# Converting 64-bit weights to 32 bits: one of three VectorE passes given to GpSimd

## Chip, cores and metric

One NeuronCore of a Trainium2 chip runs the whole kernel. The metric is the device time of one execution in microseconds. The median of three executions of the kernel before is 675.44 us (668.51 to 679.55).

## What is computed

The reference has two parts. The first is a causal attention with a memory term, for 4 batches of 8 heads, 576 rows each, head width 64, in fp32:

```python
scores = scale * np.matmul(q, k.transpose(0, 1, 3, 2))      # causal mask, softmax over the last axis
local = np.matmul(a, v)
mem_out = einsum(phi(q), M_prev) / (einsum(phi(q), z_prev) + 1e-06)
attn = g * mem_out + (1 - g) * local
```

The second is a dense layer pair on the 2304 rows of that result: `h = x @ w_in`, `g = s * relu(h)**2 + b`, `out = g @ w_out`, with w_in of 512 x 2048 and w_out of 2048 x 512. Both weight matrices arrive as 64-bit floats. TensorE takes 32-bit operands, so the kernel turns each 64-bit number into a 32-bit one on the chip before it uses it.

## The kernel before

**Conversion.** A 64-bit number arrives as two 32-bit words, `lo` and `hi`, side by side in a tile of 128 rows x 512 numbers x 2 words (`xa` for w_in, `raw` for w_out). `conv64` (lines 73 to 85) makes 32-bit floats from it. ScalarE reads `hi` as a float and scales it by a power of two, which moves the exponent to its 32-bit place (line 82). VectorE shifts the result left by three bits (line 83), brings the top three bits of `lo` in at the bottom (line 84, a shift of `lo` by 29 and an or), and sets the sign from `hi` (line 85). Line 83 reads one operand, lines 84 and 85 two each.

**Who calls it.** `split_w` converts w_in in 16 pieces of 128x512 during the first stage. After each piece, GpSimd rounds the result to the matmul's operand type (line 470, the high half) and VectorE subtracts to get the low half (line 471). `conv_u` converts w_out in 16 pieces while the last hidden-layer matmuls run; its results go through `t_u` and `split_u` on VectorE and ScalarE.

**Stages.** From 17 to 155 us the kernel handles the first four head pairs: scores on TensorE (L295, L300, L301), a masked minimum on VectorE (L314), an exponential on ScalarE (L322), the row sums' reciprocal on VectorE (L329, L330), the normalization of P on GpSimd (L334, for each head one instruction per row tile), transposes of P on TensorE (L373), and the product with V (L405 to L408). The 16 conversions of w_in are spread over this stage. The first hidden-layer matmul (L482) starts at 122 us. From 155 to 412 us attention of the later batches and hidden-layer matmuls share TensorE. From 412 to 476 us only hidden-layer matmuls are left, and w_out is converted beside them. From 477 us on the second layer runs (L744 to L746).

**What sets the order.** Every engine executes its own queue in order. The program gives the work in an order written by hand (a table of times), and a scheduler then places each instruction on its engine's queue by its own simulated times. An instruction inside `pin(...)` keeps its place relative to the other pinned ones; the others are free to move. SyncE (SP) issues the loads, also in order. A piece's load goes into one of four `xa` tiles, so load n waits until an earlier conversion has read its tile for the last time, at line 85. The loads are numbered here as the pieces are, from 0: loads 0 to 3 need no tile freed, load 7 needs the line 85 of piece 3, load 10 that of piece 7, load 11 that of piece 9, load 13 that of piece 11.

Of the kernel before, what the change touches and what calls it, by code (L numbers as in the profile page):

```python
# [12 lines left out]
ALU = mybir.AluOpType  # L13
# [18 lines left out]
def attention_moe_kernel(  # L32
# [15 lines left out]
    nc = tc.nc  # L48
# [26 lines left out]
    def conv64(raw, w, pin=lambda x: x):  # L75

        lo, hi = raw[:, :, 0], raw[:, :, 1]  # L80
        wu = w.bitcast(U32)
        pin(nc.scalar.activation(w, hi.bitcast(F32), AF.Abs, scale=2.0 ** -112))
        pin(nc.vector.tensor_scalar(wu, wu, 3, None, ALU.logical_shift_left))
        nc.vector.scalar_tensor_tensor(wu, lo, 29, wu, ALU.logical_shift_right, ALU.bitwise_or)
        nc.vector.scalar_tensor_tensor(wu, hi, 0x80000000, wu, ALU.bitwise_and, ALU.bitwise_or)


# [46 lines left out]
    pin = tc.keep_in_program_order  # L134
# [326 lines left out]
    def split_w(n):  # L461
        c, p = divmod(n, NP)
        cs = slice(512 * (c % 2), 512 * (c % 2) + 512)
        w = ap1.tile([128, 512], F32, tag="w", name="w", bufs=2)
        conv64(st.pop(("wst", n)), w, pin if PINC else same)
        H, L = (t[:, p, cs] for t in W[c // 2])
        if T["wa"][n]:
            nc.scalar.copy(H, w)
        else:
            nc.gpsimd.tensor_scalar(H, w, 1.0, 1.0, ALU.mult, ALU.mult)  # L470
        nc.vector.tensor_sub(L, w, H.bitcast(F32))
# [179 lines left out]
    def conv_u(n):  # L651
        i, h = divmod(n, 2)
        if h == 0:
            st["b"] = stage(i)
        w, s = st["b"]
        conv64(st.pop(("u", n)), w[:, 2 * h:2 * h + 2].rearrange("p a b -> p (a b)"))
        if n in NEXT:
            for r in NEXT[n]:
                load_u(r)
        if h == 0:  # L660
            return
        later(2, t_u, i, w, s)
        later(4, split_u, i, w, s)
# [223 lines left out]
```

## Time and profile before

| | |
|---|---|
| median of 3 executions | 675.44 us |
| the profiled execution | 674.27 us |
| its span, first to last instruction | 672.5 us |
| mean granted TensorE clock | 0.982 |
| busy: TensorE, VectorE, ScalarE, GpSimd | 634.5, 485.1, 469.0, 356.6 us |

The page of the profile gives each engine's busy time over the whole span. The stages differ: TensorE is busy all the time from 412 to 470 us, and less so in the first stage, where its matmuls wait for the other engines. So the windows are read by stage, then the waits inside a stage, then the lines. PE is TensorE, DVE VectorE, ACT ScalarE, POOL GpSimd, and SP the queue of SyncE that issues the loads.

### The profile page before, as it was taken

Reading aid. Unit: us, or ns where it says so; the run is one execution under the profiler, and the core shown is the slowest. Engines: PE = TensorE matmul, PEld = TensorE weight load, DVE = VectorE, ACT = ScalarE, POOL = GpSimd, SP = SyncE. Lnnn points to the kernel's source line nnn. Section 1 sums busy time; section 2 is a strip of 40 time slices with the busy share of each in tenths; the row PEclk is TensorE's granted clock in tenths of the full one; section 3 lists DMA queues with packets and bytes.
Section 4 is the critical chain, followed back from the end, with each engine's and each line's share of the span. In section 5 each row is a group of like instructions: output and inputs, shape, how many; then the busy total and the mean of one; then the engine's idle time right before and its main releaser. Section 6 shows DMA issues by size and latency. Waiting matters only on the chain. (4 is left out here: it accounts for less than half of the span.)

```text
span 672.5 us, 12998 instructions
## 1 busy us (share of the span) xinstructions
PE 634.5 (94%) x4536; PEld 575.9 (86%) x4536; DVE 485.1 (72%) x1109; ACT 469.0 (70%) x1053; POOL 356.6 (53%) x370
## 2 busy tenths in 40 slices
PE   5989799979999999999999999999899999999998
PEld 3545455869999999898998999999899998899998
DVE  4987778889677767866767653985977875568574
ACT  5677585767777767767767754769898768686841
POOL 1745556557646656654755331000577656665683
PEclk9998797999999999999999999999999999999999
DMA  7986876767778697786875564656653443434201
GB/s 268 267 232 156 177 189 157 200 170 209 190 204 214 173 231 194 201 220 173 204 189 133 140 221 142 212 189 235 227 150 118 131 137 98 125 95 156 95 25 40
DMA packets 73442, 115.75 MB, mean 172 GB/s; under 512 B 10016, under 2 KB 51232, under 8 KB 73376
## 3 DMA queue, kind: packets, MB, share of 16 engines
q1 hardware_dynamic: 71200, 112.55, 60.6%
q10 hardware_dynamic: 2176, 2.36, 1.0%
q8 instruction: 36, 0.59, 0.4%
q14 instruction: 30, 0.25, 0.1%
HBM read 57.68 MB, written 23.59 MB: 121 GB/s over the span
## 5 line engine op out<-in xcount | busy, mean ns | idle before, releaser
L334 POOL TENSOR_SCALAR P<-P,sm,omg 128x64 f32<-128x64 f32 (+4 forms) x136 | 94.7, 710 | 61.1 <-DVE sm L330 40.5
L322 ACT ACTIVATE P<-P,mn 128x64 f32<-128x64 f32 (+4 forms) x160 | 89.5, 560 | 36.1 <-DVE mn L314 35.5
L746 PE MATMUL yps<-bH,op 128*128 128x256 f32 x360 | 102.3, 285 | 2.9 <-DVE op L736 2.9
L744 PE MATMUL yps<-bH,op 128*128 128x256 f32 x360 | 101.9, 283 | 0.8 <-ACT r L491 0.8
L745 PE MATMUL yps<-bL,op 128*128 128x256 f32 x360 | 101.8, 283 | 0.0
L314 DVE CUSTOM_DVE_ANT_0 P<-sps,mask 128x64 f32<-128x64 f32 (+4 forms) x160 | 65.9, 423 | 28.8 <-PE sps L301 22.3
L373 PE MATMUL tps<-ident,P 128*128 128x128 f32 (+2 forms) x480 | 75.3, 278 | 4.7 <-POOL P L334 3.1
L482 PE MATMUL hps<-xs,w1H 128*128 128x320 f32 (+1 forms) x256 | 77.7, 304 | 0.9 <-DVE ptl L225 0.5
L482 PE MATMUL hps<-xs,w0H 128*128 128x320 f32 (+1 forms) x256 | 78.5, 307 | 0.0
L484 PE MATMUL hps<-xs,w0L 128*128 128x320 f32 (+1 forms) x256 | 75.9, 297 | 0.0
L484 PE MATMUL hps<-xs,w1L 128*128 128x320 f32 (+1 forms) x256 | 75.8, 296 | 0.0
L483 PE MATMUL hps<-xs,w0H 128*128 128x320 f32 (+1 forms) x256 | 75.8, 296 | 0.0
L483 PE MATMUL hps<-xs,w1H 128*128 128x320 f32 (+1 forms) x256 | 75.7, 296 | 0.0
L746 PEld LDWEIGHTS yps<-bH,op 128*128 128x128 f32 x360 | 68.5, 191 | 4.0 <-DVE op L736 3.9
L744 PEld LDWEIGHTS yps<-bH,op 128*128 128x128 f32 x360 | 68.6, 190 | 1.0 <-ACT r L491 1.0
L745 PEld LDWEIGHTS yps<-bL,op 128*128 128x128 f32 x360 | 68.6, 190 | 0.0
L373 PEld LDWEIGHTS tps<-ident,P 128*128 128x128 f32 (+2 forms) x480 | 55.2, 133 | 14.8 <-issue 5.9
L491 ACT ACTIVATE r<-hps 128x320 f32<-128x320 f32 (+1 forms) x128 | 50.5, 407 | 23.7 <-PE hps L484 14.6
L300 PE MATMUL sps<-X 128*128 128x192 f32 (+1 forms) x180 | 61.0, 342 | 4.7 <-DVE mn L314 4.6
L730 POOL TENSOR_TENSOR sum<-w0L 128x512 f32<-128x512 f32 x11 | 18.0, 1634 | 69.9 <-ACT w0L L713 47.8
L301 PE MATMUL sps<-X 128*128 128x192 f32 (+1 forms) x180 | 55.0, 310 | 0.0
L736 POOL TENSOR_TENSOR op<-w0L,op 128x512 fp32r<-128x512 f32 x30 | 43.2, 1458 | 18.4 <-PE hps L484 10.2
(136 smaller groups left out, 1930.0 us busy)
## 6 DMA issues: line engine op xcount, KB each, us to landing
X<-sqk SPq DMA_DIRECT2D x60, 432.0 KB, 6.1
r_d<-r SPq DMA_DIRECT2D x28, 320.0 KB, 3.6
qks<-in_qk_t_dram SPq DMA_DIRECT2D x15, 576.0 KB, 6.2
xa<-in_moe_w_in_dram SPq DMA_DIRECT2D x16, 512.0 KB, 6.8
raw<-in_moe_w_out_dram SPq DMA_DIRECT2D x16, 512.0 KB, 4.9
w1L<-r_d SPq DMA_DIRECT2D x16, 512.0 KB, 4.5
r_d<-r SPq DMA_DIRECT2D x28, 256.0 KB, 3.5
Q<-sqp SPq DMA_DIRECT2D x48, 144.0 KB, 4.3
```

The source lines that it names most:

```text
L300: nc.tensor.matmul(ps[:, :m], lhsT=lhsT, rhs=X[:, 1, c0:c0 + m], start=True, stop=False)
L301: nc.tensor.matmul(ps[:, :m], lhsT=lhsT, rhs=X[:, 2, c0:c0 + m], start=False, stop=True)
L314: nc.vector.tensor_tensor_reduce(P[:, PO[i] + c0:PO[i] + c0 + n], ps[:, :n], mask[:, mo:mo + n], -SCALE, init, ALU.add, ALU.min, mn[:, o:o ...
L322: nc.scalar.activation(pt, pt, AF.Exp, scale=-1.0, bias=mn[:, o:o + 1], accum_out=sm[:, i:i + 1])
L334: dve("nm", x // 2, i).tensor_scalar(pt, pt, sm[:, i:i + 1], omg[:, h:h + 1], ALU.mult, ALU.mult)
L373: nc.tensor.transpose(ps[0:kn, o:o + qn], P[0:qn, c:c + kn], ident[0:qn, 0:qn])
L482: nc.tensor.matmul(ps, lhsT=wH[:, p, fs], rhs=xs[:, 0], start=p == 0, stop=False)
L483: nc.tensor.matmul(ps, lhsT=wH[:, p, fs], rhs=xs[:, 1], start=False, stop=False)
L484: nc.tensor.matmul(ps, lhsT=wL[:, p, fs], rhs=xs[:, 0], start=False, stop=p == NP - 1)
L744: nc.tensor.matmul(ps, lhsT=H, rhs=BH, start=f == 0, stop=False)
L745: nc.tensor.matmul(ps, lhsT=H, rhs=BL, start=False, stop=False)
L746: nc.tensor.matmul(ps, lhsT=L, rhs=BH, start=False, stop=f == KF - 1)
```

## The change

Line 83 now runs on GpSimd and works on `lo`, in place: it reads the low word as an unsigned integer, multiplies it by about 2**-29 and adds about -0.5, and writes the result back as an unsigned integer, which leaves the top three bits as a number from 0 to 7. Line 84 on VectorE then shifts ScalarE's result left by three bits and ors that number in, in one pass over two operands. Line 85 is as before. So each of the 32 pieces has two VectorE passes where it had three, and one GpSimd pass where it had none.

```diff
         lo, hi = raw[:, :, 0], raw[:, :, 1]
         wu = w.bitcast(U32)
         pin(nc.scalar.activation(w, hi.bitcast(F32), AF.Abs, scale=2.0 ** -112))
-        pin(nc.vector.tensor_scalar(wu, wu, 3, None, ALU.logical_shift_left))
-        nc.vector.scalar_tensor_tensor(wu, lo, 29, wu, ALU.logical_shift_right, ALU.bitwise_or)
+        nc.gpsimd.tensor_scalar(lo, lo, 2.0 ** -29 * (1.0 - 2.0 ** -20), 7.5 * 2.0 ** -20 - 0.5, ALU.mult, ALU.add)
+        pin(nc.vector.scalar_tensor_tensor(wu, wu, 3, lo, ALU.logical_shift_left, ALU.bitwise_or))
         nc.vector.scalar_tensor_tensor(wu, hi, 0x80000000, wu, ALU.bitwise_and, ALU.bitwise_or)
```

The GpSimd pass isn't pinned, and it needs nothing but its load. The scheduler moves it on GpSimd's queue, and with it much else on every queue up to 400 us and again from 400 to 480 us.

GpSimd's queue around the normalization of head 2 (the third group of five L334 rows; heads are numbered from 0), before:

```order
L470 TENSOR_SCALAR w0H<-w 128x512 x2
L451 TENSOR_SCALAR xs<-x_345 128x256
L334 TENSOR_SCALAR P<-P,sm,omg 128x64
L334 TENSOR_SCALAR P<-P,sm,omg 128x192
L334 TENSOR_SCALAR P<-P,sm,omg 128x320
L334 TENSOR_SCALAR P<-P,sm,omg 128x448
L334 TENSOR_SCALAR P<-P,sm,omg 128x576
```

The same place with the change:

```order
L470 TENSOR_SCALAR w0H<-w 128x512
L83 TENSOR_SCALAR xa<-xa 128x512 x3
L470 TENSOR_SCALAR w0H<-w 128x512
L83 TENSOR_SCALAR xa<-xa 128x512
L470 TENSOR_SCALAR w0H<-w 128x512
L334 TENSOR_SCALAR P<-P,sm,omg 128x64
L334 TENSOR_SCALAR P<-P,sm,omg 128x192
L334 TENSOR_SCALAR P<-P,sm,omg 128x320
L334 TENSOR_SCALAR P<-P,sm,omg 128x448
L334 TENSOR_SCALAR P<-P,sm,omg 128x576
```

Ahead of head 2's five rows stood the high halves (L470) of pieces 1 and 2 and one xs row; now the high halves of pieces 2, 3 and 4 stand there, and the new passes over loads 4 to 7. With the change, a new pass also stands directly ahead of the group of head 1 (load 3), of head 5 (load 10), of head 8 (load 13), and one row ahead of the group of head 7 (load 11).

VectorE's queue at the same time, before, from just ahead of head 2's reciprocal (L330) to the ends of pieces 3 and 4 (the two L85 rows):

```order
L84 SCALAR_TENSOR_TENSOR w<-xa,w 128x512
L330 RECIPROCAL sm<-sm 128x5
L216 RECIPROCAL nrm<-nrm 128x10
L84 SCALAR_TENSOR_TENSOR w<-xa,w 128x512
L85 SCALAR_TENSOR_TENSOR w<-xa,w 128x512
L314 ISA P,mn<-sps,mask 128x448
L314 ISA mn 128x1
L217 TENSOR_TENSOR qs<-qs,nrm 128x640
L314 ISA P,mn<-sps,mask 128x320
L314 ISA mn 128x1
L452 TENSOR_TENSOR xs<-x_345,xs 128x256
L85 SCALAR_TENSOR_TENSOR w<-xa,w 128x512
```

And with the change, from the end of piece 3 (the first L85) to the reciprocal of head 2 (L330):

```order
L85 SCALAR_TENSOR_TENSOR w<-xa,w 128x512
L314 ISA P,mn<-sps,mask 128x288
L314 ISA mn 128x1
L471 TENSOR_TENSOR w0L<-w,w0H 128x512
L84 SCALAR_TENSOR_TENSOR w<-w,xa 128x512
L314 ISA P,mn<-sps,mask,mn 128x288
L314 ISA mn 128x1
L314 ISA P,mn<-sps,mask 128x64
L314 ISA mn 128x1
L85 SCALAR_TENSOR_TENSOR w<-xa,w 128x512
L329 TENSOR_SCALAR sm<-sm 128x5
L330 RECIPROCAL sm<-sm 128x5
```

Before, head 2's reciprocal stood ahead of the last passes of pieces 3 and 4. Now it stands behind both, with ten rows between the last pass of piece 3 and it.

GpSimd's queue at the end of the attention, before:

```order
L451 TENSOR_SCALAR xs<-x_5058 128x256
L452 TENSOR_TENSOR xs<-x_5058,xs 128x256
L451 TENSOR_SCALAR xs<-x_5069 128x320
L452 TENSOR_TENSOR xs<-x_5069,xs 128x320
L730 TENSOR_TENSOR sum_5262<-w0L 128x512
L736 TENSOR_TENSOR op<-w0L,op 128x512 x2
```

With the change:

```order
L451 TENSOR_SCALAR xs<-x_5058 128x256
L452 TENSOR_TENSOR xs<-x_5058,xs 128x256
L451 TENSOR_SCALAR xs<-x_5069 128x320
L452 TENSOR_TENSOR xs<-x_5069,xs 128x320
L83 TENSOR_SCALAR raw<-raw 128x512 x16
L730 TENSOR_TENSOR sum_5262<-w0L 128x512
L736 TENSOR_TENSOR op<-w0L,op 128x512 x2
```

All 16 new passes over w_out stand in a row, ahead of the first sum of the second layer (L730).

## Rows read from the trace of the kernel before

**Rows 1.** The page, part 1: busy us (share) xinstructions by engine.

```profile
PE 634.5 (94%) x4536; PEld 575.9 (86%) x4536; DVE 485.1 (72%) x1109; ACT 469.0 (70%) x1053; POOL 356.6 (53%) x370
```

**Rows 2.** Windows: length, busy us (instructions) by engine, clock, DMA share, GB/s.

```profile
17.00:155.00 138.00, 123.31 (x637) 84.53 (x636) 112.84 (x293) 92.08 (x243) 78.45 (x95) 0.93 0.78 195
...
412.00:470.00 58.00, 58.00 (x440) 58.00 (x440) 45.63 (x97) 43.80 (x87) 2.25 (x3) 1.00 0.61 204
470.00:505.00 35.00, 32.28 (x257) 31.88 (x256) 30.65 (x36) 31.34 (x52) 22.54 (x14) 0.95 0.62 181
```

**Rows 3.** Waits, 17 to 155 us: total us, times, longest us.

```profile
POOL P L334 <- DVE sm L330: 28.6, 4, 17.3
ACT P L322 <- DVE mn L314: 14.5, 17, 2.5
...
PE sps L300 <- DVE mn L314: 3.7, 5, 1.1
```

**Rows 4.** Lines, DVE, 17 to 155 us: xcount | busy us, mean ns.

```profile
L85 DVE SCALAR_TENSOR_TENSOR w<-xa,w 128x512 uint32<-128x512 uint32 x16 | 12.5, 779 | 0.0
L84 DVE SCALAR_TENSOR_TENSOR w<-xa,w 128x512 uint32<-128x512 uint32 x16 | 12.4, 774 | 0.1
L83 DVE TENSOR_SCALAR w<-w 128x512 uint32<-128x512 uint32 x16 | 8.7, 546 | 0.5 <-ACT w L82 0.5
L471 DVE TENSOR_TENSOR w0L<-w,w0H 128x512 fp32r<-128x512 f32 x8 | 7.4, 926 | 2.6 <-POOL w0H L470 2.6
...
L314 DVE CUSTOM_DVE_ANT_0 P<-sps,mask 128x288 f32<-128x288 f32 x11 | 4.9, 448 | 1.8 <-PE sps L301 1.8
```

**Rows 5.** Lines, DVE, whole run: the conversions of w_out.

```profile
L84 DVE SCALAR_TENSOR_TENSOR stg<-raw,stg 128x512 uint32<-128x512 uint32 x16 | 10.8, 684 | 0.0
L85 DVE SCALAR_TENSOR_TENSOR stg<-raw,stg 128x512 uint32<-128x512 uint32 x16 | 10.8, 683 | 0.0
...
L83 DVE TENSOR_SCALAR stg<-stg 128x512 uint32<-128x512 uint32 x16 | 6.7, 421 | 4.1 <-ACT stg L82 4.0
```

**Rows 6.** Lines, POOL, whole run.

```profile
L232 POOL TENSOR_TENSOR sqk<-qks,sqk 128x576 fp32r<-128x576 f32 x12 | 23.3, 1940 | 12.1 <-ACT sqk L235 11.6 <-POOL V L288 0.4
...
L470 POOL TENSOR_SCALAR w1H<-w 128x512 fp32r<-128x512 f32 x8 | 4.9, 618 | 16.4 <-DVE w L85 13.2 <-DVE sm L329 2.4 <-DVE sm L330 0.7
```

**Rows 7.** Tile xa, its loads: us from issue to landing.

```profile
DMA to landing us min/median/max: 3.8/6.8/11.8
```

**Rows 8.** Timeline, SP: start us, us, instruction; load 3 of xa.

```profile
21.88 0.41 SPq L458 DMA_DIRECT2D xa<-in_moe_w_in_dram  x1
```

**Rows 9.** Timeline, POOL: normalizations of heads 1, 2, 5, 7, 8.

```profile
26.97 5.31 POOL L334 TENSOR_SCALAR P<-P,sm,omg 128x64 f32<-128x64 f32 x5 [2.06 <-DVE sm L330]
...
41.48 4.63 POOL L334 TENSOR_SCALAR P<-P,sm,omg 128x64 f32<-128x64 f32 x5
...
76.19 4.39 POOL L334 TENSOR_SCALAR P<-P,sm,omg 128x64 f32<-128x64 f32 x5
...
99.11 2.59 POOL L334 TENSOR_SCALAR P<-P,sm,omg 128x192 f32<-128x192 f32 x4
...
110.86 2.37 POOL L334 TENSOR_SCALAR P<-P,sm,omg 128x64 f32<-128x64 f32 x4
```

**Rows 10.** Timeline, PE: first transposes of P of heads 2, 5, 7 and 8.

```profile
45.37 0.66 PE L373 MATMUL tps<-ident,P 128*128 128x128 f32 x4 [1.40 <-POOL P L334]
...
81.37 1.06 PE L373 MATMUL tps<-ident,P 128*128 128x128 f32 x4
...
104.53 1.99 PE L373 MATMUL tps<-ident,P 128*128 128x128 f32 x15
...
117.45 0.60 PE L373 MATMUL tps<-ident,P 128*128 128x128 f32 x4
```

**Rows 11.** Timeline, PE, the second wait after the last hidden-layer matmul.

```profile
484.32 0.38 PE L746 MATMUL yps<-bH,op 128*128 128x256 f32 x1 [1.97 <-DVE op L736]
```

**Rows 12.** Timeline, DVE, the low halves of the late operands.

```profile
477.34 5.72 DVE L689 TENSOR_TENSOR w1H<-late,w0H 128x1024 fp32r<-128x1024 f32 x4
```

## Prediction

> **What bounds the kernel now.** The page comes first: TensorE (PE) is busy 94% of the span, VectorE (DVE) 72%, GpSimd (POOL) 53% [rows 1]. That average hides three stages, so the windows come next [rows 2]. From 412 to 470 us, where the second half of the conversions runs, PE is busy for all 58.00 us and POOL for 2.25: PE alone sets that stage. From 17 to 155 us, where the first half runs, PE is busy 123.31 of 138 us at a granted clock of 0.93, a mean of stretches at 2.4 and at 1.2 GHz, while DVE is busy 112.84 us (82%) and POOL 78.45 (57%). There PE waits for the chain score, minimum, exponential, reciprocal, normalization, transpose. The waits of that stage show DVE in it three times: PE's scores wait 3.7 us for the minimum, ScalarE's exponential 14.5 us, and POOL's normalization 28.6 us for the reciprocal, 17.3 of it before the first head [rows 3]. So only the first stage can give time back, and DVE and POOL are both in its chain.
>
> **What the change takes from DVE.** In the first stage the three passes of a piece cost 546, 774 and 779 ns [rows 4], together 2.10 us, or 33.6 us for 16 pieces. Beside an idle POOL the same passes cost 421, 684 and 683 ns [rows 5], together 1.79. So POOL's work beside them, 57% of the stage, makes them 17% longer. Removing line 83 saves 16 x 0.546 = 8.7 us. The new line 84 reads two operands, one of them a low word of every pair, as the old one did; I leave its price at 0.774.
>
> **What it gives to POOL.** No row shows POOL reading and writing unsigned integers. Its pass over 128x512 dense floats takes 618 ns, its longest kind of pass (two operands, 128x576) 1940 ns [rows 6]. The new pass has one operand, so it is nearer the first; the conversions and the stride lie on top. I take 0.9 us, and keep 0.62 and 1.94 as ends; cheaper than the dense pass over as many numbers I exclude. In the first stage that is 16 x 0.9 = 14.4 us, so POOL's 57% becomes 67%. By the proportion of the rows, the 17% becomes 20%: the two passes left rise by 16 x 2 x 0.02 us = 0.6 us, and the other 79.2 us of DVE, if all of it suffers alike, by 2.3 us. DVE's net gain is 8.7 - 2.9 = **5.8 us**. What of it reaches the end lies between nothing (PE's waits end elsewhere) and all of it (DVE paces the stage). DVE has 18% of idle time, but it releases the largest waits, so I take half: **-2.9 us**.
>
> **What stands in POOL's queue.** The new pass waits for its load, and POOL executes in order, so the normalizations behind it wait too. Five heads have such a pass directly or nearly ahead: 1, 2, 5, 7 and 8. For head 2 it is load 7, which can't be issued before the last pass of piece 3 frees its tile. A load lands 3.8 to 11.8 us after its issue, 6.8 in the median [rows 7]. With 0.1 us for the issue and 0.9 for the pass, POOL is past it 7.8 us after piece 3. In the new order ten DVE rows and then head 2's reciprocal stand behind piece 3. Their costs (two passes of 774 and 779 ns, one of 926, two of about 0.45 to 0.5, the rest under 0.3 each) [rows 4] make 4.4 us. So the normalization is 3.4 us later than its reciprocal allows. The same count gives 5.7, 4.9 and 4.8 us of DVE work for heads 5, 7 and 8, and delays of 2.1, 2.9 and 3.0 us. Head 1 waits for load 3, issued at 21.88 us [rows 8]: 21.88 + 6.8 + 0.9 = 29.6, where its normalization began at 26.97 [rows 9], so 2.6 us.
>
> Not all of this reaches PE. Head 2's transposes began at 45.37 us, before its normalization had ended (41.48 + 4.63 = 46.11): no slack, which I take for head 1 too. Heads 5, 7 and 8 had 0.8, 2.8 and 4.2 us between the end of the one and the start of the other [rows 9, 10]. What is left is 2.6 + 3.4 + 1.3 + 0.1 + 0 = 7.4 us. PE's order was also rearranged, with other work ahead of some transposes, and DVE catches up in such gaps, so I take half: **+3.7 us**. The ends: nothing, if loads land in 3.8 us; all of it at 11.8 us, where the delays are 7.6, 8.4, 7.1, 7.9 and 8.0, less 7.8 of slack, 31.2 us.
>
> **Other places.** From 412 to 470 us DVE loses 16 x 0.421 = 6.7 us of work and POOL gains 14.4 where it was idle; PE's 58.00 of 58 covers both. If that cover went, PE would have to wait for DVE, whose 45.63 us leave 12.4 free. Behind this stage PE waits 1.97 us for an operand [rows 11] which stands in DVE's queue behind four passes of 5.72 us together [rows 12]. These write into a tile that the last hidden-layer matmul frees, so faster conversions don't move them: 0, within 2 us either way. The first sum of the second layer now stands behind the 16th new pass on POOL; its operands go through this same wait, within the same bound. ScalarE and the sizes of all loads are unchanged.
>
> **The sum.** -2.9 + 3.7 = +0.8 us on the profiled execution of 674.27 (span 672.5 and 1.8 around it), so 675.1. The median of the runs lies 1.2 us above that execution: **676 us**.
>
> **The rivals.** *DVE paces the first stage and the loads are in time.* For it speaks DVE's 82%; against it, that the scheduler put the passes by its own load times, and the trace's loads vary threefold. It gives 674.27 - 5.8 = 668.5, a median of 670. If PE's idle 14.7 us and its stretches at 1.2 GHz shrink with it, more: a clock of 0.93 over 138 us is at most 9.7 us, and over half of these 24.4 us would have to come back for a gain of 2%. 0.22, of which 0.08 for the gain beyond 2%.
>
> *The loads hold up the normalizations in full* (the other side). Its place is POOL's queue ahead of heads 1, 2, 5, 7 and 8; its price grows with the landing. For it speaks that PE waited 1.40 us for head 2's normalization already [rows 10], and that PE falls to 1.2 GHz in this stage; against it, that POOL has 59.5 us free. At a landing of 9.3 us, between median and longest, the delays are 5.1, 5.9, 4.6, 5.4 and 5.5, less 7.8 of slack, 18.7 us; with -2.9 that is +15.8: 690, a median of 691. It passes 2% where the delays that reach PE exceed 16.4 us, at a landing of about 8.8 us for all five. 0.17.
>
> *DVE and POOL shut each other out.* The rows show both running together, with DVE's passes 17% longer. Were each new POOL pass instead to stop DVE for its whole 0.9 us, DVE would lose 14.4 us and save 8.7 in the first stage: +5.7, and with the +3.7 of the loads 683.7, a median of 685, not beyond 2%. The Trainium skill says this in "SBUF — State Buffer", section "Who interferes with whom": a VectorE instruction with two SBUF inputs and a GpSimd instruction that reads SBUF exclude each other, and the later one blocks fully. By that rule the gain turns into a loss; the 17% at 57% of POOL time speaks for a partial cost, since most DVE work beside POOL shows no such stretch. 0.10.
>
> *The pass does more than it says.* Above 1.94 us per pass, four of the five delays grow by over 1 us each. It adds 4 to 8 us to the forecast and is inside the range: 0.03.
>
> **Chances and range.** The forecast, no change beyond 2%, has 0.48; with the rivals' shares, 0.08 faster by over 2%, 0.75 within, 0.17 slower. 2% is 13.5 us, about what a measurement of this kernel can tell, whose three runs span 11 us. The range reaches from 664, below the gain in full, to 690, up to the rival on the other side: 0.1 is left out on each side.
>
> **What would show it.** DVE's busy time in the first stage falls by about 6 us, and line 84 costs near 0.8 us; over 1.3 us would be the shutting out. The new POOL pass shows a mean of 0.6 to 1.9 us. POOL's waits gain a row on the loads of xa, of some 10 to 15 us in total; its absence would make the first rival right. PE's waits for P grow from a few us in the first stage; the first hidden-layer matmul, at 122 us now, comes within 4 us of that. Wrong would be a wait of PE between 412 and 470 us, or a difference that arises after 155 us.

## The result

The changed kernel takes 679.32 us (median of 4 executions, 675.91 to 682.7) where the kernel before takes 671.98 in the same comparison: a ratio of 1.0144, 95% interval 1.0099 to 1.0189. (The ratios leave out slow executions, those over 1.5% above the fastest of their kernel, so they are not the quotients of the medians.) That is 1.4% slower, less than 2%. The forecast's time, its range and its class hold. The loss itself is some 7 us between the medians and 10 us by the ratio, where 0.8 us was forecast, and the runs below show that it comes in the main from elsewhere.

### The profile page after: what moved, and what is told of

Its sections match the earlier page's. It is cut to its first block, busy times and chain, and to the rows that moved or that the text cites. A ratio compares the mean times of both kernels' runs of the same rounds, so it can differ in the third digit from the quotient of the medians.

```text
span 677.2 us, 13026 instructions
## 1 busy us (share of the span) xinstructions
PE 633.9 (94%) x4536; PEld 575.5 (85%) x4536; DVE 473.0 (70%) x1077; ACT 468.9 (69%) x1053; POOL 384.8 (57%) x402
## 5 line engine op out<-in xcount | busy, mean ns | idle before, releaser
L334 POOL TENSOR_SCALAR P<-P,sm,omg 128x64 f32<-128x64 f32 (+4 forms) x136 | 91.5, 685 | 40.1 <-ACT V L287 17.4
L300 PE MATMUL sps<-X 128*128 128x192 f32 (+1 forms) x180 | 60.9, 343 | 10.6 <-DVE mn L314 9.2
L225 DVE TENSOR_TENSOR ptl<-tps,pth 128x512 fp32r<-128x512 f32 (+1 forms) x72 | 41.8, 595 | 15.9 <-ACT pth L221 12.9
L736 POOL TENSOR_TENSOR op<-w0L,op 128x512 fp32r<-128x512 f32 x30 | 41.5, 1401 | 17.5 <-ACT op L735 17.3
```

What stands on the lines that cost most here:

```text
L300: nc.tensor.matmul(ps[:, :m], lhsT=lhsT, rhs=X[:, 1, c0:c0 + m], start=True, stop=False)
L334: dve("nm", x // 2, i).tensor_scalar(pt, pt, sm[:, i:i + 1], omg[:, h:h + 1], ALU.mult, ALU.mult)
```

## The profile after

The profiled execution took 679.01 us (span 677.2, mean granted clock 0.979). The page's part 1, busy time by engine, answers [rows 1]:

```profile
PE 633.9 (94%) x4536; PEld 575.5 (85%) x4536; DVE 473.0 (70%) x1077; ACT 468.9 (69%) x1053; POOL 384.8 (57%) x402
```

VectorE has 12.1 us less to do and GpSimd 28.2 more. The windows answer [rows 2]; the first one ends at the first hidden-layer matmul, so that it holds the same TensorE work in every kernel below:

```profile
17.00:126.94 109.94, 93.83 (x428) 56.45 (x426) 79.82 (x207) 69.11 (x180) 67.45 (x87) 0.91 0.76 194
...
17.00:155.00 138.00, 119.15 (x615) 80.45 (x614) 102.22 (x267) 90.06 (x236) 84.53 (x109) 0.93 0.74 188
...
412.00:470.00 58.00, 58.00 (x433) 58.00 (x432) 44.23 (x84) 38.32 (x80) 23.88 (x21) 1.00 0.67 217
470.00:505.00 35.00, 30.14 (x232) 29.93 (x231) 24.01 (x29) 31.41 (x55) 16.22 (x11) 0.90 0.52 161
```

The same window of the kernel before, up to its first hidden-layer matmul:

```profile
17.00:122.13 105.13, 94.19 (x427) 57.49 (x426) 85.65 (x222) 70.09 (x184) 60.57 (x75) 0.90 0.79 194
```

TensorE idles there for the window less its busy time: 10.9 us before, 16.1 with the change. The first hidden-layer matmul starts at 126.94 us instead of 122.13, 4.8 us later, about the whole difference of the two profiled executions (674.27 and 679.01). Each profile is one execution: the same work with the same queues, profiled again as e8 below, reached that matmul at 132.70. From 412 to 470 us TensorE is busy all the time, as before. TensorE's own waits in the first window (total us, times, longest):

```profile
PE sps L300 <- DVE mn L314: 6.2, 7, 1.4
PE ops L405 <- ACT x L435: 3.9, 3, 2.5
PE tps L373 <- POOL P L334: 2.5, 3, 1.5
```

Before, in its window:

```profile
PE ops L405 <- ACT x L435: 5.5, 3, 3.3
PE tps L373 <- POOL P L334: 1.9, 2, 1.4
...
PE sps L300 <- DVE mn L314: 1.7, 3, 1.0
```

The row to look at is that of the scores (L300). They wait 6.2 us, in seven places, for VectorE's masked minimum, which frees the score bank in PSUM; before, it was 1.7 us in three. The transposes' wait for P, where the forecast looked for the loss, is 2.5 us instead of 1.9.

GpSimd's new pass, by its two places (xcount | busy us, mean ns | idle before):

```profile
L83 POOL TENSOR_SCALAR raw<-raw 128x512 uint32<-128x512 uint32 x16 | 20.1, 1256 | 25.8 <-DMA raw<-in_moe_w_out_dram 9.9 <-DVE stg L671 8.4 <-DVE stg L85 6.8
...
L83 POOL TENSOR_SCALAR xa<-xa 128x512 uint32<-128x512 uint32 x16 | 13.0, 811 | 27.7 <-DMA xa<-in_moe_w_in_dram 24.6 <-DVE mn L314 2.7
```

It does wait for its loads ahead of the normalizations. For head 2, GpSimd's timeline shows the pass and the normalization behind it:

```profile
47.62 0.64 POOL L83 TENSOR_SCALAR xa<-xa 128x512 uint32<-128x512 uint32 x1 [5.62 <-DMA xa<-in_moe_w_in_dram]
...
48.94 3.50 POOL L334 TENSOR_SCALAR P<-P,sm,omg 128x64 f32<-128x64 f32 x5
```

and VectorE's timeline the reciprocal that this normalization needs:

```profile
45.10 0.19 DVE L330 RECIPROCAL sm<-sm 128x5 f32<-128x5 f32 x1
```

From 45.10 to 48.94 us are 3.84 us, of which the reciprocal takes 0.19. So the normalization is some 3.7 us late, where 3.4 was forecast. It was real; the runs below show that it is not what cost the time.

## The experiments

Four theories stood against each other. A, mine: the new pass waits for its load in GpSimd's in-order queue, ahead of normalizations of the first stage. B: the pass itself costs, by its time or by contention. C: the scheduler, given less VectorE work, lays every queue anew, and the new order costs. D: the loss comes from the second place, w_out. Ratios are to runs of the kernel before on the same chip at the same time. There are three such groups, e1 to e4, e5 to e8 and e9 to e12, each on a chip of its own; the kernel before has medians of 666.00, 667.82 and 669.97 us in them, so times compare within a group and ratios between groups. "Old order" is the order of every engine's queue in the kernel before, "new order" that in the changed kernel.

**Each place alone (e1: w_in, e2: w_out).**

```diff
-        conv64(st.pop(("wst", n)), w, pin if PINC else same)
+        conv64(st.pop(("wst", n)), w, pin if PINC else same, True)   # w_in: GpSimd pass + two VectorE passes
...
+        if win:        # first run; "if not win" in the second
+            nc.gpsimd.tensor_scalar(lo, lo, 2.0 ** -29 * (1.0 - 2.0 ** -20), 7.5 * 2.0 ** -20 - 0.5, ALU.mult, ALU.add)
+            pin(nc.vector.scalar_tensor_tensor(wu, wu, 3, lo, ALU.logical_shift_left, ALU.bitwise_or))
+        else:
+            pin(nc.vector.tensor_scalar(wu, wu, 3, None, ALU.logical_shift_left))
+            nc.vector.scalar_tensor_tensor(wu, lo, 29, wu, ALU.logical_shift_right, ALU.bitwise_or)
```

> The GpSimd pass for the 16 pieces of w_in alone; w_out keeps its three VectorE passes. Theory A (the new pass waits for its load in GpSimd's in-order queue, ahead of normalizations of the first stage): the whole loss stays, a ratio of 1.010 to 1.019 to before, first hidden-layer matmul near 127 us. Rival B (GpSimd's passes slow VectorE beside them, wherever they stand): part of the loss, since half of the passes are gone; in the first stage the same 127 us. Rival D (the loss comes from the second place, the 16 passes ahead of the second layer's first sum): 1.000 +- 0.003.

> The GpSimd pass for the 16 pieces of w_out alone; w_in keeps its three VectorE passes. Theory A: 1.000 +- 0.003 to before, first hidden-layer matmul at 122 us, since TensorE covers that stage; a wait of up to 5 us behind the hidden layer is possible by the order of ScalarE's queue. Rival B: the same or up to 1.005. Rival D: 1.010 to 1.019.

With w_in alone: 682.72 us, ratio 1.0221 (1.0166 to 1.0277), above the 1.010 to 1.019 that theory A gave it, first hidden-layer matmul at 133.36 us. With w_out alone: 667.84, 1.0003 (0.9961 to 1.0046), at 122.42. So the second place costs nothing that shows, and rival D falls.

**The GpSimd pass held back (e3), and no GpSimd pass (e4).** Both edits are shown against the changed kernel; `zlo` is a zero, one element per partition.

```diff
-        nc.gpsimd.tensor_scalar(lo, lo, ...)
+        pin(nc.gpsimd.tensor_scalar(lo, lo, ...))        # e3
```

```diff
-        nc.gpsimd.tensor_scalar(lo, lo, ...)
-        pin(nc.vector.scalar_tensor_tensor(wu, wu, 3, lo, ALU.logical_shift_left, ALU.bitwise_or))
+        pin(nc.vector.scalar_tensor_tensor(wu, wu, 3, zlo.broadcast_to((128, 512)), ALU.logical_shift_left, ALU.bitwise_or))   # e4
```

> Both places have the GpSimd pass, but in w_in it is held at its place in the hand-written order, behind the GpSimd instructions written before it, so that it can't stand ahead of an earlier normalization by the scheduler's load times. Same work on every engine. Theory A: GpSimd's waits for the loads of xa fall from 15.7 us to under 6, first hidden-layer matmul at 122 us or before (116 to 122), ratio 0.990 to 1.000 to before. Rival B (cost and contention of the pass): as the change, 1.010 to 1.019. Rival C (any new order of the queues costs this much, whatever stands in them): between 1.00 and 1.02, without relation to the load waits.

> Two VectorE passes and no GpSimd pass: a zero of one element per partition, broadcast, stands in for the low word, so the top three bits of the low word are left out of the weights. Theories A and B: VectorE's gain alone, 2.9 to 5.8 us, a ratio of 0.991 to 0.996; first hidden-layer matmul at 116 to 120 us. Rival C: no gain or a loss, 1.00 to 1.015, since the queues are in a new order here too. If VectorE's time is worth nothing in this stage: 1.000 +- 0.002.

The held pass gives 679.97 us, ratio 1.0198 (1.0135 to 1.0261), first hidden-layer matmul at 128.98. Its waits from 17 us to there:

```profile
PE ops L405 <- ACT x L435: 9.2, 4, 3.8
...
PE sps L300 <- DMA X<-sqk: 5.1, 3, 2.1
...
POOL xa L83 <- DMA xa<-in_moe_w_in_dram: 3.2, 2, 2.3
```

GpSimd's wait for the loads has nearly gone, from 14.5 us in the same part of the changed kernel to 3.2, and the loss is still there. That speaks against theory A. It doesn't settle it, since the waits of TensorE are others now: this is a third order of the queues, which may have a price of its own.

Without any GpSimd pass, and with one VectorE pass less for each piece, the kernel takes 679.76 us, 1.0166 (1.0098 to 1.0234). Less work on one engine and, but for one memset of 128x1, no more on any other makes it slower, so the pass can't be the whole cause. Theory C explains it: the scheduler lays all queues anew. This run's profiled execution is its fastest (673.48 us, first hidden-layer matmul at 119.25), so its trace doesn't show where this order loses.

**Work and order apart.** All these kernels trace the same instructions in the same sequence, so an order can be given as a list of positions in it. A table taken from one kernel's schedule then holds the queues of another:

```diff
+def in_order(tc):
+    order = ...                     # positions in the traced sequence, in the order of the other kernel
+    ins = ...                       # the instructions as traced
+    last = {}
+    for n in order:
+        i = ins[n]
...
+        e = str(i.engine)
+        if e in last:               # issue order only, no wait for the other to finish
+            tc.add_manual_dep(i, last[e].name, mybir.DependencyInfo(
+                mybir.DependencyClass.NoSync, mybir.DependencyReason.DATA), reason="in_order")
+        last[e] = i
...
         attention_moe_kernel(tc, *args)
+        in_order(tc)
```

The five runs, in the order of their expectations: the new work in the old order (e5), the old work in the new order (e6), no GpSimd pass in the old order (e7), and as controls the new work in the new order (e8) and the old work in the old order (e12).

> The changed kernel's instructions, but each engine's queue held to the order of the kernel before by a table; the 32 GpSimd passes stand where the removed VectorE passes stood in that order. TensorE, ScalarE and SyncE have exactly the queues of before. Theory C (the scheduler lays every queue anew for the shorter VectorE work, and that new order is what costs): 0.990 to 1.003 to before, first hidden-layer matmul at 116 to 122 us. Theory A (load waits in GpSimd's queue): between, 0.995 to 1.010, since the new passes stand behind more normalizations here. Rival B (cost and contention of the GpSimd pass): as the change, 1.010 to 1.019.

> The instructions of the kernel before, three VectorE passes and none on GpSimd, but each engine's queue held to the order of the changed kernel; the first pass stands directly ahead of the second. Theory C: slower than before by at least the change's own loss, 1.012 to 1.03, first hidden-layer matmul at 126 us or later, though no GpSimd pass exists. Theories A and B: 1.000 to 1.005, since no new pass waits, costs or contends.

> Two VectorE passes, no GpSimd pass (the low word's top three bits are left out of the weights), in the order of the kernel before. Theory C: VectorE's gain alone, 0.985 to 1.000, where the same work in its own new order was 1.017. If the order does not matter: 1.010 to 1.023 again.

> Control: the changed kernel held to its own order by the same kind of table. All theories: the change's own result, 1.010 to 1.025; another value would mean that the table itself costs time.

> Control: the kernel before held to its own order by the same kind of table. All theories: 0.997 to 1.003, score waits of 1 to 3 us in the first stage, as in the other runs in this order.

| work \ order | old | new |
|---|---|---|
| three VectorE passes (before) | 1.0018 (0.9977 to 1.0058) | 1.0160 (1.0111 to 1.0208) |
| two VectorE passes, no GpSimd pass | 1.0017 (0.9981 to 1.0054) | |
| two VectorE passes and the GpSimd pass | 1.0094 (1.0060 to 1.0128) | 1.0208 (1.0159 to 1.0256) |

The controls, e12 at the upper left and e8 at the lower right, show no cost of the table itself: the first is at 1 (a cost of up to 0.6% stays inside its interval), the second overlaps the change's own 1.0099 to 1.0189. The upper row is the main finding: **the old work in the new order is 1.6% slower**, with no GpSimd pass in it that could wait for a load, cost or contend. Its first hidden-layer matmul is at 125.14 us, a little before the 126 that was expected.

Down the right column, the GpSimd pass with all its load waits, and VectorE's pass gone, add 0.5%, and the two intervals overlap. Down the left column VectorE's pass removed gives no gain that shows (1.0017; its interval excludes one above 0.2% if the table is free, and against the control about 0.5% would still fit), and the GpSimd pass added costs 0.8%, about 5 us (the medians of e5 and e7 are 3.7 us apart). So e5 lies above the 1.003 that theory C allowed by itself: the order and the pass both have a part. And the pass costs no more where it waits for its loads than where, in the first stage of e5, it hardly does, so theory A falls.

VectorE's gain isn't lost everywhere. In the one profiled execution each, the runs with two VectorE passes for w_in in the old order (e5, e7, e9) reach the first hidden-layer matmul at 117.75 to 118.99 us, those with three (before, e2, e11, e12) at 121.43 to 122.42. Why the ratios show nothing of these 3 to 4 us stays open.

TensorE's waits from 17 us to the first hidden-layer matmul show what the order does. The old work in the new order:

```profile
PE sps L300 <- DVE mn L314: 7.4, 7, 1.7
PE ops L405 <- ACT x L435: 3.0, 3, 1.4
PE tps L373 <- POOL P L334: 1.5, 1, 1.5
```

and in the old order:

```profile
PE tps L373 <- POOL P L334: 2.9, 3, 1.4
PE sps L300 <- DVE mn L314: 2.4, 3, 1.1
PE ops L405 <- ACT x L435: 2.4, 2, 1.6
```

The scores' wait for the minimum is 7.4 us against 2.4, in seven places against three, as in the changed kernel (6.2, seven). One such place on TensorE's timeline, old work in the new order:

```profile
37.81 0.40 PE L300 MATMUL sps<-X 128*128 128x288 f32 x1
38.05 0.29 PE L301 MATMUL sps<-X 128*128 128x288 f32 x1
38.19 0.38 PE L252 MATMUL tps<-ident,qs 128*128 128x128 f32 x2
38.33 0.38 PE L300 MATMUL sps<-X 128*128 128x288 f32 x1
38.55 0.29 PE L301 MATMUL sps<-X 128*128 128x288 f32 x1
38.67 0.38 PE L252 MATMUL tps<-ident,qs 128*128 128x128 f32 x2
40.30 0.36 PE L300 MATMUL sps<-X 128*128 128x192 f32 x1 [1.24 <-DVE mn L314]
```

and the first scores of that head in the old order:

```profile
37.53 0.64 PE L252 MATMUL tps<-ident,qs 64*128 64x64 f32 x3
37.92 0.34 PE L300 MATMUL sps<-X 128*128 128x192 f32 x1
38.10 0.27 PE L301 MATMUL sps<-X 128*128 128x192 f32 x1
38.30 0.75 PE L405 MATMUL ops<-sqp,V 64*64 64x320 f32 x2
38.89 0.70 PE L406 MATMUL ops<-pt,V 64*64 64x320 f32 x2
39.52 0.86 PE L408 MATMUL ops<-pth,V 128*64 128x256 f32 x4
```

The kernel has two score banks (`ps_s`, two buffers). In the new order three score tiles stand close together with only short transposes between them, so the third waits 1.24 us for VectorE to empty a bank. In the old order products with V stand there, and nothing waits. The changed kernel waits at the same score, 0.98 us at 41.72 (shown at the end). That the waits for a bank follow from the order is shown by the two rows of waits; that they are all of its price up to this matmul is not: a third bank for the scores was not tried.

Over the whole first part the idle time of TensorE is the window less its busy time (columns as above). Old work in the old order, then in the new:

```profile
17.00:122.02 105.02, 95.90 (x428) 58.51 (x426) 84.25 (x221) 70.26 (x184) 62.21 (x75) 0.92 0.77 194
```

```profile
17.00:125.14 108.14, 94.95 (x427) 57.44 (x425) 85.22 (x220) 68.76 (x180) 60.39 (x75) 0.92 0.77 196
```

Idle are 9.1 us against 13.2; in the changed kernel it is 16.1 (109.94 - 93.83). The granted clock of the two stretches is the same, 0.92.

The whole price is larger than this pair of executions shows. They lie 4.7 us apart (674.93 and 679.63), at nearly the same mean clock (0.982 and 0.980). The median of the old work in the new order and that of the kernel before beside it lie 10.5 us apart (678.27 and 667.82), at median clocks of 0.9785 and 0.989. At the same clocks, 0.977 to 0.982, four executions of the one average 676.95 us and six of the other 671.81: 5.1 us (7.2 if the three longest of the six are left out, as the ratios do). So, as an estimate from these few, 5 to 7 of the 10.5 us are there at the same clock, and the rest comes with a lower clock. Whether the order's waits are what lowers it was not tried.

**Which half of the order (e10, e11).** With `old` and `new` for the two orders, the table of e10 holds

```python
new[:1000] + [i for i in old if i not in new[:1000]]      # old and new exchanged in e11
```

> The work of before (three VectorE passes), all queues in the order of the changed kernel up to the first hidden-layer matmul (the first 1000 instructions), in the order of before from there. If the order costs in the first stage (TensorE's scores wait for VectorE's minima): 1.011 to 1.021, first hidden-layer matmul at 125 us or later, score waits of 5 us or more. If it costs at the transition behind the hidden layer: 1.000 to 1.004.

> The mirror image: the work of before, the order of before for the first 1000 instructions, the order of the changed kernel from there. First stage: 1.000 to 1.004, first hidden-layer matmul at 118 to 123 us. Transition: 1.011 to 1.021.

The new order up to the first hidden-layer matmul: 679.51 us, 1.0142 (1.0087 to 1.0197), with score waits of 7.3 us in seven places. The new order from there: 673.98, 1.0056 (1.0015 to 1.0097). So more of the loss comes from the first stage than from behind it (the two intervals just overlap). In that second part, the first matmul of the second layer waits longer, here in the run with the new order from the hidden layer:

```profile
482.51 0.58 PE L744 MATMUL yps<-bH,op 128*128 128x256 f32 x1 [5.17 <-ACT r L491]
```

It waited 0.75 us in the profile of before, and 1.97 us followed [rows 11]. The changed kernel has 4.86 in this place.

**What the GpSimd pass costs by itself (e9).** The pass is executed, but written behind the piece's VectorE passes; a zero stands in for the low word's top bits in e4, e7 and here, so no VectorE pass needs its result.

```diff
         nc.vector.scalar_tensor_tensor(wu, hi, 0x80000000, wu, ALU.bitwise_and, ALU.bitwise_or)
+        nc.gpsimd.tensor_scalar(lo, lo, ...)
```

> As the run without the GpSimd pass in the old order (the zero stands in for the low word), but the 32 GpSimd passes are executed, each placed behind the last VectorE pass of its piece: the same GpSimd work in the same stage, whose load has long landed and whose result nobody waits for; only the tile's release for the next load waits for it. If the 0.8% between the two runs in the old order is VectorE waiting for the pass: 1.000 to 1.004 to before. If it is the pass's own time and contention, which delay the normalizations and VectorE: 1.007 to 1.013.

677.44 us, 1.0103 (1.0067 to 1.0139): the same as with the pass ahead (1.0094). The edit does less than was expected of it. The pass stands later in the program, but nothing ties it to VectorE's passes, so it runs when GpSimd comes to it: in the trace 10 of the 16 passes over w_in, and all 16 over w_out, start before the last VectorE pass of their piece, and some still wait for their load. Piece 3, on GpSimd and on VectorE:

```profile
36.16 0.70 POOL L89 TENSOR_SCALAR xa<-xa 128x512 uint32<-128x512 uint32 x1 [2.69 <-DMA xa<-in_moe_w_in_dram]
```

```profile
41.76 0.68 DVE L88 SCALAR_TENSOR_TENSOR w<-xa,w 128x512 uint32<-128x512 uint32 x1
```

What the run shows is that the price doesn't need VectorE to wait for the pass's result. In e5 VectorE does wait for it from 17 to 155 us, in e9 it can't, and the ratio is the same. In e5, first that wait, then the line of the pass itself, which has as good as no wait for loads:

```profile
DVE w L84 <- POOL xa L83: 5.2, 4, 1.8
```

```profile
L83 POOL TENSOR_SCALAR xa<-xa 128x512 uint32<-128x512 uint32 x15 | 12.5, 833 | 1.4 <-DMA xa<-in_moe_w_in_dram 0.2
```

So the 0.8% goes with the pass being there. One thing moves with it: VectorE's low halves, which need GpSimd's high halves. Without the pass (e7), then with the late pass (e9) (line, xcount | busy us, mean ns | idle before), 17 to 155 us:

```profile
L475 DVE TENSOR_TENSOR w0L<-w,w0H 128x512 fp32r<-128x512 f32 x8 | 5.7, 712 | 0.9 <-POOL w0H L474 0.9
```

```profile
L475 DVE TENSOR_TENSOR w0L<-w,w0H 128x512 fp32r<-128x512 f32 x8 | 7.9, 987 | 4.3 <-POOL w0H L474 4.3
```

The first half's low halves wait 4.3 us for GpSimd instead of 0.9, and one of them takes 987 ns instead of 712. This can't be the whole price: in the profiled executions e9 and e5 start the first hidden-layer matmul at 118.73 and 118.99 us, only 1.0 and 1.2 us behind e7. Where the rest of the 5 us arises isn't shown. No version tried is faster than the kernel before: two VectorE passes for w_out alone (1.0003) come nearest.

**How VectorE and GpSimd meet.** Why one pass can take 0.7 us and the next 1.5 is in the timelines. In the traces of before and of the change a two-operand VectorE pass of the conversion (lines 84 and 85) with no GpSimd instruction beside it takes 0.67 to 0.69 us. Where the two overlap, one waits for the other. In the changed kernel GpSimd's pass began first, and VectorE's took 1.13 us:

```profile
16.30 1.16 POOL L83 TENSOR_SCALAR xa<-xa 128x512 uint32<-128x512 uint32 x1 [3.74 <-DMA xa<-in_moe_w_in_dram]
```

```profile
16.87 1.13 DVE L84 SCALAR_TENSOR_TENSOR w<-w,xa 128x512 uint32<-128x512 uint32 x1
```

Here VectorE's began first and took its 0.69 us, and GpSimd's took 1.10 where it takes 0.64 to 0.67 undisturbed:

```profile
75.70 0.69 DVE L84 SCALAR_TENSOR_TENSOR w<-w,xa 128x512 uint32<-128x512 uint32 x1
```

```profile
75.82 1.10 POOL L83 TENSOR_SCALAR xa<-xa 128x512 uint32<-128x512 uint32 x1 [0.17 <-DMA xa<-in_moe_w_in_dram]
```

In the first pair VectorE's pass ends 0.54 us after GpSimd's. So it is with all passes that were stretched in these two traces by more than 0.05 us: they end 0.52 to 0.55 us after the GpSimd instruction that ran when they began, whatever that one's length. Over the 64 passes this adds 3.0 us before and 6.6 us with the change.

## Why the prediction was right in its number and wrong in its working

- **What the change takes from DVE (-2.9 us).** The busy time fell as reckoned: from 85.65 us to the first hidden-layer matmul before (the window 17 to 122.13 us) to 79.82, that is -5.8. But "half taken" for what reaches the end isn't borne out: in the same order no gain shows (1.0017, from 0.9981 to 1.0054; -2.9 us would be 0.9957). The profiled executions do reach the hidden layer 3 to 4 us earlier, so the step that is in doubt is the way from there to the end, and its cause is open.
- **What stands in POOL's queue (+3.7 us).** The waits for loads came (15.7 us in eight places to 155 us; 10 to 15 forecast), and so did the delay of head 2 (3.7 us; 3.4 forecast). The step that failed is that they reach TensorE: its transposes waited 1.9 us for P before, to the first hidden-layer matmul, and 2.5 after; with the load waits down to 3.2 us the loss stayed (1.0198), and the pass adds 0.5% in the order with these waits and 0.8% in the one nearly without.
- **PE's rearranged order.** The prediction named it as relief ("DVE catches up in such gaps") and priced it at nothing. It is the largest term: 1.6% (1.1 to 2.1), 10.7 us on 667.8; the new order up to the first hidden-layer matmul alone gives 1.4%.
- **The GpSimd pass.** Its price of 0.9 us was near (0.81 for w_in, 1.26 for w_out), but the sum held only VectorE's stretch and the load waits against it. In the old order its presence costs 0.8%, about 5 us, of which the profiled executions show some 1 us at the first hidden-layer matmul.
- **412 to 470 us: 0**, as forecast: TensorE 58.00 of 58, and w_out alone at 1.0003. **The transition: 0 within 2 us.** The one wait of 4.86 us took the place of 0.75 and 1.97, so 2.1 us more, at the bound. That no difference arises after 155 us was too much: the second part of the order costs 0.56% (0.15 to 0.97).
- **The rivals.** *DVE paces the first stage* falls, since no gain shows at the end. *The loads hold up the normalizations in full* falls with the held pass and with the right column of the table. *DVE and POOL shut each other out*: the mechanism is there, the price isn't. Where a two-operand VectorE pass and a GpSimd instruction overlap, one waits for the other. The rule of the Trainium skill ("SBUF — State Buffer", "Who interferes with whom"), an exclusive lock by which the later of the two is blocked, agrees with these rows: VectorE's passes end 0.52 to 0.55 us after the GpSimd instruction ahead of them. But few passes meet one, so lines 84 and 85 lose 3.6 us more over both places, where this rival took 14.4 us for the first stage alone. The prediction read its 17% as a partial cost; it is the mean of undisturbed passes and of passes that wait. For the same reason its sign, a mean of line 84 over 1.3 us, couldn't show the lock: the mean of 812 ns hides passes of 0.68 and of 1.49 us.

The parts add up to 1.6 + 0.8 + 0 = 2.4%, above the change's 1.44% (1.0 to 1.9) and in the interval of its control run (1.6 to 2.6). The forecast of +0.8 us was a small loss from two terms of which neither shows at the end, in place of two that it lacked. That 676 us came near 679.32 is luck as well: it was counted from 674.27 us, above the medians of 666.0 to 672.0 us that the kernel before had in every later comparison.

## What to carry to other kernels

Where a scheduler lays the queues by simulated times, an edit's price has two parts, the work and the new order, and the second can be the larger; compare the queue of the engine that bounds the stage before and after, and count where score tiles, banks or buffers now follow each other too closely. Hold the order fixed to measure the work alone: here that turned a change that seemed to cost 1.4% by its load waits into nothing that shows for VectorE, 0.8% for GpSimd and 1.6% for the order. A mean that lies above the undisturbed time can be a mixture: look at single passes and at what the other engine did at that moment. And a wait that grows as forecast on an engine off the path is no evidence that it costs: look at the waits of the engine that sets the end.

## What the runs showed of the hardware

- Executions of one kernel differ in the TensorE clock that is granted, and their times with it: the kernel before took 662.9 to 664.3 us at a mean of 0.995 to 0.997, and 667.9 to 674.8 at 0.977 to 0.982, in the group of e5 to e8. In the new order the median clock is lower: 0.9785 for the old work and 0.9735 for the new work, against 0.989 for before. In the changed kernel TensorE waited four times, 3.6 us together, from 38 to 43.6 us:

```profile
38.48 0.40 PE L300 MATMUL sps<-X 128*128 128x288 f32 x1 [0.71 <-DVE mn L314]
...
40.30 0.44 PE L252 MATMUL tps<-ident,qs 128*128 128x128 f32 x2 [0.80 <-ACT pth L356]
41.72 0.53 PE L300 MATMUL sps<-X 128*128 128x192 f32 x1 [0.98 <-DVE mn L314]
...
43.56 1.11 PE L405 MATMUL ops<-sqp,V 64*64 64x256 f32 x2 [1.09 <-ACT x L435]
```

  and the granted clock over 40 to 50 us is 0.66, so a part of it at 1.2 GHz and a part at 2.4:

```profile
40.00:50.00 10.00, 7.62 (x22) 3.95 (x23) 5.48 (x17) 5.48 (x17) 2.92 (x5) 0.66 0.70 172
```

  The old work in the old order has 1.00 there, and 0.69 from 60 to 70 us.
- A one-operand GpSimd pass over 128x512 unsigned integers, every second word, took 0.64 to 0.67 us undisturbed, 0.81 in the mean over w_in, and 1.26 in the mean over w_out, where one of the 16 took 6.1 us while VectorE's passes followed each other.
- VectorE's two-operand passes and GpSimd's instructions took turns where they overlapped: VectorE's took 0.67 to 0.69 us alone and up to 1.9 us (in the kernel before) behind a GpSimd instruction that had begun first.
